# Batch 0 of an FFT filter ahead of an MLP: i moved into a second inverse table, angles by an integer shift, filters in three parts, another order

## The chip, the core and the metric

The kernel runs on one core of a Trainium2 chip. The metric is the device time of one execution in microseconds (us). The profile shows five engines: TensorE (PE in the profile, with its weight loads PEld), VectorE (DVE), ScalarE (ACT), GpSimd (POOL) and SyncE (SP). A program on one core has no second core to compare with, so each execution is judged by its time and by its mean granted TensorE clock, where 1.000 is full speed.

## The reference, cut to what matters

```python
x = randn(8, 3008, 256) * 0.1                     # batch, sequence, channels
F = filt_r + 1j * filt_i                          # (1505, 256)
y = irfft(rfft(x, axis=1) * F, n=3008, axis=1)    # a global filter along the sequence
h = y.reshape(24064, 256) @ w_in                  # 256 -> 2048
g = 0.5 * h * (1 + erf(h / sqrt(2)))
out = g @ w_out                                   # 2048 -> 256, fp32
```

## The kernel before

The Fourier transform of 3008 points is done by tables: 3008 = 47 x 64, so a first transform over 47 (table T1), a second over 64 with the twiddles in its table (T2), the product with the filter, and the way back (T3, T4). The tables are computed on the chip as sines. Batch 0 is transformed entirely in SBUF before the MLP can start (c1, c1t, c2, product, c3, c3t, c4); batches 1 to 7 are transformed in between the matmuls of the MLP (s1, r1, s2, s3, r2, s4, with a trip through DRAM). Here each engine works through its own instructions in the order in which the program lists them. Of the tiles named below, at is what c1 leaves, b its transposes (c1t), which c2 reads, p the filtered products, vt what c3 leaves, d its transposes (c3t), which c4 reads, and y the result; for batches 1 to 7, d is loaded back from DRAM (R).

The angles of T2 are kept in turns. The program brings them between -0.5 and 0.5 before the sine: they are rounded by adding and subtracting a large number, and the rounded part is subtracted:

```python
def table_2_angle(self, h):
    v, k = self.nc.vector, K1 // 2
    w, r = self.gen[:, h], self.gen[:, 2]
    if h == 0:
        v.scalar_tensor_tensor(out=w, in0=kk..., scalar=self.n2, in1=jn..., op0=ALU.mult, op1=ALU.add)
    else:
        v.tensor_scalar(out=w, in0=self.gen[:, 0], scalar1=self.n12, scalar2=None, op0=ALU.add)
    v.tensor_scalar(out=r, in0=w, scalar1=RND, scalar2=-RND, op0=ALU.add, op1=ALU.add)
    v.tensor_tensor(out=w, in0=w, in1=r, op=ALU.subtract)

def table_2_sin(self, h):
    self.nc.scalar.activation(out=self.T2[:, 12 * h:12 * h + 12, 1, :], in_=self.gen[:, h], func=AF.Sin, scale=2.0 * PI)
```

The second transform yields z, and the filter needs z*fr + (i z)*fi. T2 holds three blocks a row, so that c2 computes z and i z by two sets of matmuls in two PSUM banks; one VectorE instruction multiplies both by the two parts of the filter, and c3 adds the two halves by accumulating two matmuls with the same weights T3:

```python
def c2(self, p):
    ...
    for t, o in ((0, 1), (1, 0)):                  # z, then i z
        for i in range(2):
            k = 2 * p + i
            nc.tensor.matmul(ps[:, t, 256 * i:256 * i + 256], lhsT=self.T2[:, k, o:o + 2]...,
                             rhs=self.st[0, "b", k // 4][:, k % 4, :], start=True, stop=True)
    f = self.F[:, :, 2 * p:2 * p + 2, :]
    if p < 11:
        nc.vector.tensor_tensor(out=w, in0=ps, in1=f.rearrange("p t a b -> p t (a b)"), op=ALU.mult)
        return
    ...                                            # the last product in two halves

def c3(self, p, np=2):
    ...                                            # for t in (0, 1):
    self.nc.tensor.matmul(ps[half][:, c:c + 128], lhsT=w[:, t, o:o + 128],
                          rhs=self.T3[:, 2 * (p + i) + k]..., start=t == 0, stop=t == 1)
```

The filters come by DMA into the lower 64 partitions in parts of rows, and GpSimd (for the first rows VectorE) copies them to the upper 64. The order of the start-up, with cuts:

```python
m.load_x(0, 0, 1, (0,)); ...; m.load_x(0, 1, 4)    # x of batch 0
m.table_2(g); m.table_2_angle(0); m.unit_matrices(g, cols); m.table_2_angle(1)
for k, n in ((0, 4), (4, 4), (8, 8), (16, 8)):
    m.load_filters(k, n)
m.dup_filters(nc.gpsimd, 4, 4)
m.load_w_in()                                      # two large DMA issues between the copies
m.dup_filters(nc.gpsimd, 8, 8)
for u in range(16):
    m.c1(u // 2, u % 2, act if u < 4 or u % 2 else False)
    if u == 3:
        m.warm_up(3); m.table_2_sin(0)
    ...
nc.scalar.activation(out=warm, in_=m.p, func=AF.Gelu)   # brings the Gelu table
m.c1t(0, False); m.c1t(1, act)
...
m.c2(0); m.c2(1); m.table_3(0, act); m.table_2_swap(1); m.c1t(2, act)
for q in range(1, 7):
    ...                                            # c2, c1t, c2, tables, c3
m.psum(wide, v=(5, 1), t=(3, 1))                   # PSUM banks of c4 and c3t
for u in range(10):
    ...                                            # c3t(u), c4(u - 2)
...
# batches 2 to 7, in slots of the MLP counted back from the batch's first slot hi:
s1, n1, r1, s2, n2, r2, s4, n4 = hi - 94, 3.5, hi - 80, hi - 69, 3.5, hi - 24, hi - 17, 1
```

`warm_up(n)` is n matmuls on a tile of ones whose result nobody reads; they only keep TensorE busy.

## Time and profile before

| | before |
|---|---|
| time, median of 3 runs | 774.69 us (774.12 to 776.34) |
| span of the profiled execution | 772.2 us |
| first sine of T2 | 8.38 us |
| first filter product | 16.72 us |
| last product ends | 32.02 us |
| first matmul of the MLP | 40.55 us |

The page, the busy time by stretch and the main links of the start-up are in the prediction below. Here are four more lines of the timeline of the kernel before (columns: start us, length us, engine, line, operation, output<-input, shapes, count, and in brackets the idle time just before with what ended it):

```profile
5.75 1.01 DVE L179 SCALAR_TENSOR_TENSOR gen<-kk,n,jn 128x768 f32<-128x768 f32 x1
6.79 0.56 DVE L183 TENSOR_SCALAR gen<-gen 128x768 f32<-128x768 f32 x1
...
8.38 0.84 ACT L187 ACTIVATE T<-gen 128x768 bf16<-128x768 f32 x1 [0.18 <-DVE gen L184]
...
40.55 0.59 PE L461 MATMUL ps_h<-y_sb,w_in_sb 128*128 128x512 bf16 x2 [0.73 <-DMA x_sb<-in_x_dram]
```

The sine at 8.38 waits for the subtraction (L184). The MLP starts at 40.55; its wait is put down to a load of x, but the last eviction of y ends within the same 0.73 us.

### The profile page before, as it was taken

What the parts mean: (1) busy time and instruction counts of PE and PEld (TensorE: products, weight loads), DVE (VectorE), ACT (ScalarE), POOL (GpSimd) and SP (SyncE); (2) the same over time, 40 slices, a digit from 0 to 9 for tenths busy, and PEclk for the clock granted to TensorE, in tenths of its full rate; (3) what the DMA queues carried; (4) which work ended last, traced back from release to release, by engine and by line L of the source; (5) the groups of instructions that cost most, each with busy time, mean ns of one, the idle gap of its engine ahead of it and who ended that gap; (6) DMA issues with size and microseconds to landing.
All of it is one profiled execution on the core that took longest, in us unless ns stands there. A gap on an engine that the chain in (4) does not pass through costs nothing.

```text
span 772.2 us, 15059 instructions
## 1 busy us (share of the span) xinstructions
PE 763.2 (99%) x6066; PEld 528.7 (68%) x6066; DVE 397.3 (51%) x722; ACT 567.4 (73%) x981; POOL 64.9 (8%) x160
## 2 busy tenths in 40 slices
PE   8999999999999999999999999999999999999998
PEld 4847675676776766677777776666776776766666
DVE  7866755464555645457463664637646366411011
ACT  6879955897568975699656996579865798666663
POOL 7801100020000200011000110001100000000000
PEclk9999999999999999999999999999999999999999
DMA  8894745466253661636516464255553422410111
GB/s 138 145 180 124 150 123 129 128 124 151 57 139 107 138 159 41 192 78 122 143 53 181 85 133 123 79 154 95 124 137 81 139 83 69 123 42 28 42 42 55
DMA packets 87398, 85.66 MB, mean 111 GB/s; under 512 B 6752, under 2 KB 77536, under 8 KB 87328
## 3 DMA queue, kind: packets, MB, share of 16 engines
q1 hardware_dynamic: 78816, 68.70, 31.0%
q0 software_dynamic: 8512, 16.00, 14.9%
q8 instruction: 47, 0.77, 0.4%
q14 instruction: 23, 0.19, 0.1%
HBM read 54.00 MB, written 46.66 MB: 130 GB/s over the span
## 4 chain that ended last, share of the span: by engine, by line
PE 94%; DMA 3%; POOL 2%; issue 0%; DVE 0%; POOLq 0%
PE ps_o L488 43%; PE ps_h L461 42%; PE ps_s L345 2%; PE ps_s L320 2%; PE ps_s L295 2%; PE ps_s L272 2%; DMA x_sb<-in_x_dram 2%; POOL F L96 1%; POOL x_sb L82 1%; DMA F<-in_filt_i_dram 1%; POOL F L91 0%; PE ps_e L478 0%; POOL T1s L258 0%; DVE ost L501 0%; POOL T1p L580 0%
## 5 line engine op out<-in xcount | busy, mean ns | idle before, releaser
L464 ACT ACTIVATE g_sb<-ps_h 128x512 bf16<-128x512 f32 x752 | 438.0, 597 | 182.8 <-PE ps_h L461 172.1
L488 PE MATMUL ps_o<-w_out_sb,g_sb 128*128 128x256 bf16 x2992 | 447.5, 273 | 0.0
L461 PE MATMUL ps_h<-y_sb,w_in_sb 128*128 128x512 bf16 (+3 forms) x1600 | 445.8, 366 | 0.7 <-DMA x_sb<-in_x_dram 0.7
L488 PEld LDWEIGHTS <-g_sb 128*128 128x128 bf16 x2992 | 283.9, 98 | 134.3 <-issue 9.9
L461 PEld LDWEIGHTS <-w_in_sb 128*128 128x128 bf16 x1600 | 154.7, 98 | 23.7 <-issue 1.1
L494 DVE COPY ost<-ps_o 128x512 f32<-128x512 f32 x93 | 63.8, 686 | 143.5 <-PE ps_o L488 143.4
L303 DVE TENSOR_TENSOR p<-ps_s,F 128x512 bf16<-128x512 f32 x84 | 58.1, 691 | 105.9 <-ACT p L302 89.5
L249 DVE TENSOR_SCALAR y_sb<-ps_s 128x376 bf16<-128x376 f32 x112 | 60.9, 548 | 80.5 <-PE ps_s L345 80.5
L247 DVE CAST a_sb<-ps_s 128x512 bf16<-128x512 f32 x112 | 69.3, 682 | 27.7 <-PE ps_s L272 27.7
L247 DVE CAST v_sb<-ps_s 128x512 bf16<-128x512 f32 x84 | 57.4, 684 | 2.9 <-PE ps_s L320 2.6
L301 ACT ACTIVATE p<-ps_s 64x512 bf16<-64x512 f32 x84 | 49.9, 594 | 2.1
L302 ACT CAST p<-ps_s 64x512 bf16<-64x512 f32 x84 | 48.5, 577 | 1.0
L345 PEld LDWEIGHTS <-d_sb 96*128 96x128 bf16 x448 | 30.8, 97 | 25.3 <-DMA d_sb<-R 0.2
L101 POOL COPY gate<-p 1x1 bf16<-1x1 bf16 x48 | 8.5, 178 | 470.3 <-DVE p L305 470.3
L305 DVE TENSOR_TENSOR p<-p 128x512 bf16<-128x512 bf16 x84 | 35.7, 425 | 2.9
L345 PE MATMUL ps_s<-T,d_sb 96*128 96x94 bf16 x448 | 36.3, 204 | 0.0
L304 DVE TENSOR_TENSOR p<-p,F 128x512 bf16<-128x512 bf16 x84 | 34.8, 415 | 0.0
L82 POOL DMA_DIRECT2D x_sb<-in_x_dram x64 | 32.7, 512 | 13.0 <-issue 12.5
L320 PE MATMUL ps_s<-p,T 128*128 128x256 bf16 x168 | 32.1, 273 | 0.0
L295 PE MATMUL ps_s<-b_sb,T 128*128 128x256 bf16 x168 | 32.1, 273 | 0.0
L320 PEld LDWEIGHTS <-T 128*128 128x128 bf16 x168 | 16.4, 98 | 20.1 <-DVE p L305 0.5
L295 PEld LDWEIGHTS <-T 128*128 128x128 bf16 x168 | 16.4, 98 | 13.4
(103 smaller groups left out, 189.1 us busy)
## 6 DMA issues: line engine op xcount, KB each, us to landing
out_dram<-ost SPq DMA_DIRECT2D x93, 256.0 KB, 2.3
x_sb<-in_x_dram POOLq DMA_DIRECT2D x64, 188.0 KB, 3.8
R<-a_sb SPq DMA_DIRECT2D x112, 96.0 KB, 2.1
b_sb<-R SPq DMA_DIRECT2D x28, 384.0 KB, 4.3
R<-v_sb SPq DMA_DIRECT2D x42, 256.0 KB, 3.5
d_sb<-R SPq DMA_DIRECT2D x56, 192.0 KB, 4.7
w_in_sb<-in_moe_w_in_dram POOLq DMA_DIRECT2D x2, 512.0 KB, 7.8
w_out_sb<-in_moe_w_out_dram POOLq DMA_DIRECT2D x2, 512.0 KB, 11.3
```

The costliest lines, as they stand in the source:

```text
L247: self.nc.vector.tensor_copy(out=out, in_=in_)
L249: self.nc.vector.tensor_scalar(out=out, in0=in_, scalar1=scale, scalar2=None, op0=ALU.mult)
L295: nc.tensor.matmul(ps[:, 256 * i:256 * i + 256], lhsT=self.T2[:, k, 1:3].rearrange("p a b -> p (a b)"), rhs=self.st[b, "b", k // 6][:, k % ...
L301: nc.scalar.activation(out=p2[0:64], in_=ps[64:128], func=AF.Copy, scale=-1.0)
L302: nc.scalar.copy(out=p2[64:128], in_=ps[0:64])
L303: nc.vector.tensor_tensor(out=p1, in0=ps, in1=f(0), op=ALU.mult)
L320: nc.tensor.matmul(ps[:, 256 * i:256 * i + 256], lhsT=self.T3[:, k].rearrange("p a b -> p (a b)"), rhs=w[:, 256 * i:256 * i + 256], start= ...
L345: nc.tensor.matmul(ps[:, 94 * i:94 * i + 94], lhsT=d[:, (grp % 2) * 4 + i, 128 * half:128 * half + 128], rhs=t4, start=True, stop=True)
L461: nc.tensor.matmul(ps[:, o:o + n], lhsT=self.w_in_sb[:, dc, jc * 128:jc * 128 + 128], rhs=self.ring[:, dc, off:off + n], start=(dc == 0), ...
L464: nc.scalar.activation(out=self.st["g", t][:, jc, :], in_=ps, func=AF.Gelu)
L488: nc.tensor.matmul(ps[:, tile_i % 2, :], lhsT=g[:, jc, tile_i * 128:tile_i * 128 + 128], rhs=self.w_out_sb[:, jc, :], start=(jc == 0), sto ...
L494: nc.vector.tensor_copy(out=ost, in_=ps)
```

## The change

The intent is to shorten the start-up of 40.5 us. Five things change together.

1. Multiplying by i moves into a second inverse table T3i. Then c2 needs one set of matmuls, the product reads one PSUM bank twice, and c3 uses T3 for one half and T3i for the other.
2. Angles carry an extra 64 turns, which makes every value a float between 64 and 128. Shifting its bits left by 15 drops sign, exponent and the six bits of whole turns. What remains, read as a signed integer, is the fraction of a turn, and the sine takes it with the scale 2 pi / 2^32.
3. Filters come in parts of 4, 8 and 12 rows: 12 transfers instead of 16.
4. w_in is loaded ahead of all filter copies.
5. The order is another one, with more warm-up matmuls and the Gelu table brought later. The loads of x, too, stand elsewhere among GpSimd's instructions (not in the excerpt), but the last is issued at nearly the same time, 5.8 us against 5.9.

```diff
-        v.tensor_scalar(out=r, in0=w, scalar1=RND, scalar2=-RND, op0=ALU.add, op1=ALU.add)
-        v.tensor_tensor(out=w, in0=w, in1=r, op=ALU.subtract)
+        ts(out=self.gen[:, 1, k].bitcast(I32), in0=w[:, k].bitcast(I32), scalar1=15, scalar2=None,
+           op0=ALU.logical_shift_left)
 ...
-        self.nc.scalar.activation(out=self.T2[:, 12 * h:12 * h + 12, 1, :], in_=self.gen[:, h], func=AF.Sin,
-                                  scale=2.0 * PI)
+        self.nc.scalar.activation(out=self.T2[:, k, 0, :], in_=self.gen[:, 1, k].bitcast(I32), func=AF.Sin,
+                                  scale=2.0 * PI / 2.0 ** 32)
 ...
+    def table_3_copy(self, q, turn):
+        v = self.t3.rearrange("p (k n r) -> p k r n", k=8, r=2)
+        self._evac(self.T3[:, 8 * q:8 * q + 8], v, "act")
+        if turn:
+            for r in range(2):
+                self._evac(self.T3i[:, 8 * q:8 * q + 8, r, :], v[:, :, 1 - r, :], "act", self.turn[r])
 ...                                               # in c2
-        for t, o in ((0, 1), (1, 0)):
-            for i in range(2):
-                nc.tensor.matmul(ps[:, t, 256 * i:256 * i + 256], lhsT=self.T2[:, k, o:o + 2]..., ...)
+        for i in range(2):
+            nc.tensor.matmul(ps[:, 256 * i:256 * i + 256], lhsT=self.T2[:, k]..., ...)
-            nc.vector.tensor_tensor(out=w, in0=ps, in1=f..., op=ALU.mult)
+            nc.vector.tensor_tensor(out=w, in0=ps.unsqueeze(1).to_broadcast([128, 2, 512]), in1=f..., op=ALU.mult)
 ...                                               # in c3
+                        t3 = (self.T3i if t else self.T3)[:, 2 * (p + i) + k]
 ...                                               # in the order
-    for k, n in ((0, 4), (4, 4), (8, 8), (16, 8)):
+    for k, n in ((0, 4), (4, 8), (12, 12)):
         m.load_filters(k, n)
-    m.dup_filters(nc.gpsimd, 4, 4)
     m.load_w_in()
-    m.dup_filters(nc.gpsimd, 8, 8)
+    m.dup_filters(nc.gpsimd, 4, 20)
 ...
+    m.c1t(0, (act, False))
+    m.table_3_copy(1, True)
+    m.c1t(1, (act,))
+    m.c2(0)
+    m.warm_up(1)
+    m.c2(1)
+    m.c1t(2, (act,))
+    m.warm_up(2)
+    for q in range(1, 7):
+        ...                                        # c2, c1t, warm_up(2), c2, c3, warm_up(1)
 ...
-    m.psum(wide, v=(5, 1), t=(3, 1))
+    m.psum(wide, v=(4, 1), t=(4, 1))
```

## The prediction

> **What bounds the kernel now.** I read first the page (engine shares and the chain that ended last), then the busy time by stage, then the start-up by its timeline, its groups and its waits. The page:
>
> ```profile
> PE 763.2 (99%) x6066; PEld 528.7 (68%) x6066; DVE 397.3 (51%) x722; ACT 567.4 (73%) x981; POOL 64.9 (8%) x160
> ...
> PE 94%; DMA 3%; POOL 2%; issue 0%; DVE 0%; POOLq 0%
> ```
>
> TensorE is busy for 99% of the span and makes 94% of the chain. The table of stretches says where the rest lies (columns: stretch, its length, busy us of PE, PEld, DVE, ACT, POOL with instruction counts, TensorE clock, DMA share, GB/s):
>
> ```profile
> 0.00:10.00 10.00, 7.15 (x44) 3.46 (x45) 7.40 (x32) 4.41 (x9) 7.74 (x25) 1.00 0.75 128
> 10.00:20.00 10.00, 8.98 (x109) 6.52 (x106) 8.70 (x14) 9.22 (x19) 8.35 (x15) 1.00 1.02 149
> 20.00:30.00 10.00, 9.43 (x129) 8.61 (x129) 8.81 (x9) 9.36 (x16) 9.71 (x14) 1.00 0.82 143
> ...
> 100.00:300.00 200.00, 200.00 (x1600) 138.85 (x1598) 109.78 (x199) 146.56 (x252) 10.96 (x32) 1.00 0.50 120
> ```
>
> From 41 us on TensorE never stops (200.00 of 200). There the change touches nothing but the stride of a weight tile (T2 holds two blocks a row, not three). So 731.6 us of the 772.2 (first matmul of the MLP at 40.55 us to the end) stay as they are, and everything is decided in the first 40.5 us: building the tables and transforming batch 0. There no single engine is full; the timeline shows who holds whom:
>
> ```profile
> 14.53 0.89 PEld L371 LDWEIGHTS <-at_sb 128*128 128x128 bf16 x16 [0.66 <-DVE at_sb L247]
> ...
> 16.72 4.82 DVE L388 TENSOR_TENSOR p<-ps_c,F 128x1024 bf16<-128x1024 f32 x4
> ...
> 22.43 6.88 DVE L388 TENSOR_TENSOR p<-ps_c,F 128x1024 bf16<-128x1024 f32 x6 [0.88 <-POOL F L96]
> ...
> 29.61 1.23 DVE L388 TENSOR_TENSOR p<-ps_c,F 128x1024 bf16<-128x1024 f32 x1 [0.30 <-POOL F L96]
> ...
> 33.69 5.56 DVE L247 COPY d_sb<-ps_c3t 96x1024 bf16<-96x1024 bf16 x8 [0.75 <-PE ps_c3t L424]
> ```
>
> Three links. (a) To 14.5 us: the first transform (c1), paced by x arriving (its last part waits for DMA at 13.09). (b) 16.72 to 32.02: twelve filter products on VectorE, back to back but for 0.88 + 0.30 us in which they wait for GpSimd to copy the filters to the upper 64 partitions (L96, ten copies of 1.04 us). (c) 32.5 to 40.4: eight VectorE copies of 0.69 us, then two evictions, and the MLP starts.
>
> **What the Trainium skill says.** "VectorE: DVE Perf Modes", section "The perf-mode tier table": a two-tensor operation runs at one element a cycle with any PSUM operand; a one-source fp32 operation in SBUF reaches twice that. The trace agrees: the product of 1024 elements takes 1217 ns (1024 / 0.96 GHz = 1067, plus a fixed part), the two-source subtract of 768 fp32 959 ns, the one-source add 560. Hence reading one PSUM bank twice by a broadcast saves VectorE nothing. "ScalarE: Activation LUTs", section "What ACT_TABLE_LOAD costs": 1283 ns a load, and about 93 ns more for a per-partition scale. The load agrees (1283 ns at L571); for the second the trace has only a hint: the 94-column T4c eviction, with such a scale, takes 357 ns. "DMA: Bandwidth & Descriptors", section "Anatomy of one DMA": some 2 us fixed per transfer beside the bytes. Filter transfers of 64 KB here take 4.1 to 5.4 us from issue to landing, queueing included, so the trace is not against it.
>
> **The change part by part.**
> 1. *Products (c2).* The multiplication by i moves from the second table to the inverse one, so c2 needs 2 matmuls a pair of rows in place of 4: 24 fewer of 256 columns, some 0.3 us less per pair (four now take 0.60 us). About 20 extra warm-up matmuls are put between, at some 0.21 us each (three in 0.81-0.84 us at full clock, with latency). TensorE gains nothing net and isn't the bound here; VectorE's products are unchanged.
> 2. *Tables.* The two round-and-subtract pairs (0.56 + 0.96 us each) become one shift each; I take 0.56 us from the one-source row, so 1.9 us less VectorE before the sines. The first sine can start near 7.2 us, not 8.38. But x still lands near 13 us, so little comes out of it.
> 3. *ScalarE before the products.* Added ahead of 14.5 us: a table-3 copy (1.02) and two swaps (0.86); taken out: two evictions (0.9). It had 0.69 + 0.44 us of idle time after 9 us, so c1 ends at 14.5 to 15.2 instead of 14.5. The first c1t is split over two engines and only eight transposes stand before it, which gives back about 0.4. First product: 16.7 to 17.0 (now 16.72).
> 4. *Filters.* 12 transfers instead of 16 save 4 x 0.54 = 2.2 us of GpSimd issue, and no w_in issue stands between the copies. Rows 4 to 11 should be there by 17.5, the first copy done at 18.6, the tenth near 28 (now 29.3). At 1.04 us a copy against 1.15 a product (6.88/6) copies stay ahead: the waits of 0.88 + 0.30 go.
> 5. *ScalarE in the products.* Out: the table load and its dummy (1.48, to the idle 2.29 us before the c4 evictions), T1q 0.35, two minus copies and two swaps 1.63, T4c 0.36. In: four turned copies of 512 elements, 0.58 + 0.09, so about 2.6. The c1t for rows 4 to 7 now stands behind the second table-3 copy and two of them: 16.45 + 1.02 + 1.3 + 1.0 = 19.75, so the third product starts at about 20.2 where VectorE is free at 19.35. A new wait of about 0.85.
>
> Sum for the end of the products: 17.0 + 2.35 + 0.85 + nine at 1.15 + 1.2 = 31.75, against 32.02: -0.3. ScalarE's own sum (16.45 + 1.0 + 1.3 + three b 3.0 + vt 1.2 + b 1.0 + vt 1.2 + b 1.0 + table 3 2.3 + four vt 4.3) ends at 32.8 against 32.58 now, so it may hold the last vt: +0.1. Link (c) has the same VectorE work: 0. Net about -0.2 to -0.3, from 774.69 to 774.4.
>
> **The rivals.** *All waits of the products vanish* (c1 ends at 14.5, the c1t isn't late): VectorE is then the only bound, first product 16.3, end near 30.2, and 1.8 us are gained: 772.9. For it: VectorE loses 1.9 us before the sines. Against it: ScalarE is at 9.2 and 9.4 of 10 us already. *ScalarE becomes the bound*: the 2.6 us of turned copies aren't covered, c3 evictions come late and c3t starts 1 us later: 775.7. For it: the same two numbers; against it: as much was taken out. *The filters come late in coarse parts*: 12 rows must all land before the thirteenth is copied; if that is after 25 us the seventh product waits, up to +1 us. Against it: all filters were in by about 22 us even with 16 issues. *The long stage is disturbed*: no; weights, sizes, order and loads are the same there.
>
> **Range and chances.** 2% is 15.5 us, over a third of the whole start-up, and no rival moves over 2 us. The three runs of before spread over 2.2 us, so the range is the rivals' and about half a microsecond: 773.0 to 775.8.
>
> **What would show it.** Right: the MLP's first matmul at 40.0 to 40.9 us; no product waiting for GpSimd; product duration still 1.22 us; a wait of 0.5 to 1.2 us before the third product, released by TensorE after ScalarE's b; the shift at about 0.56 us; the second table load inside ScalarE's idle time; 731.6 us from first MLP matmul to the end. Wrong: a shift of 0.95 us, filters after 25 us, ScalarE's last vt after 33.3, or a long stage that differs by over 0.5 us, say from a single TensorE stop of its own.

## The result

Ratios here and below are the mean time of one kernel's fast runs over the mean of the other's of the same rounds, so they are not quite the ratio of the medians quoted. Before ran in 774.95 us (median of 4, 774.12 to 776.34), after in 773.71 (median of 4, 773.30 to 774.88). The ratio is 0.9985 with a 95% interval of 0.9966 to 1.0003: the same within 2%, and not told apart from no change at all.

The page of the kernel after:

```profile
span 771.8 us, 15050 instructions
PE 763.7 (99%) x6060; PEld 527.3 (68%) x6060; DVE 397.7 (52%) x734; ACT 568.3 (74%) x980; POOL 63.0 (8%) x154
```

The shares are those of before. The busy time by stretch of the kernel after (columns as in the prediction):

```profile
10.00:20.00 10.00, 8.11 (x99) 5.70 (x97) 8.28 (x16) 9.14 (x15) 7.97 (x14) 1.00 1.15 175
20.00:30.00 10.00, 9.91 (x129) 8.14 (x127) 9.34 (x10) 8.61 (x14) 9.77 (x15) 1.00 0.67 122
```

Between 20 and 30 us TensorE is now busy for 9.91 of 10, against 9.43 before: in the stage of the products it has next to no slack left. The timeline of the kernel after, by the same links as in the prediction:

```profile
6.07 0.61 DVE L182 TENSOR_SCALAR gen<-gen 128x768 int32<-128x768 int32 x1
6.71 0.84 ACT L208 ACTIVATE T<-gen 128x768 bf16<-128x768 int32 x1 [2.28 <-DVE gen L182]
...
14.10 0.90 PEld L395 LDWEIGHTS <-at_sb 128*128 128x128 bf16 x16 [0.42 <-DVE at_sb L271]
...
15.82 2.36 DVE L412 TENSOR_TENSOR p<-ps_c,F 128x1024 bf16<-128x1024 f32 x2
...
18.39 0.38 PE L408 MATMUL ps_c<-b_sb,T 128*128 128x256 bf16 x2 [1.27 <-ACT b_sb L269]
...
18.86 7.20 DVE L412 TENSOR_TENSOR p<-ps_c,F 128x1024 bf16<-128x1024 f32 x6 [0.68 <-PE ps_c L408]
...
26.58 3.49 DVE L412 TENSOR_TENSOR p<-ps_c,F 128x1024 bf16<-128x1024 f32 x3 [0.52 <-issue]
...
32.00 1.28 ACT L637 ACT_TABLE_LOAD   x1
...
32.92 5.56 DVE L271 COPY d_sb<-ps_c3t 96x1024 bf16<-96x1024 bf16 x8 [0.75 <-PE ps_c3t L445]
...
39.24 0.55 DVE L273 TENSOR_SCALAR y_sb<-ps_c 128x376 bf16<-128x376 f32 x1 [0.22 <-PE ps_c L459]
...
39.94 0.59 PE L482 MATMUL ps_h<-y_sb,w_in_sb 128*128 128x512 bf16 x2 [0.73 <-DVE y_sb L273]
```

The first product starts 0.9 us earlier than in the first trace of before (15.82 against 16.72). No product waits for GpSimd. Instead the third waits 0.68 us, because its matmuls wait for ScalarE's copy b, and the ninth 0.52 us. The six in between take 7.20 us, against 6.88 for six before. The chain of waits of the kernel after tells who sets that pace (columns: start us, length us, what):

```profile
20.75 0.22 PE ps_warm L263
...
21.64 0.43 PE ps_warm L263 x2
...
24.06 0.43 PE ps_warm L263 x2
```

From 19.2 to 31.7 us the chain is TensorE's nearly throughout, and ten entries of it, 3.03 us together, are warm-up matmuls.

### The profile page after: what moved, and what is told of

The parts are those of the page before. It is cut to its first block, busy times and chain, and to the rows that moved or that the text cites. A ratio compares the mean times of both kernels' runs of the same rounds, so it can differ in the third digit from the quotient of the medians.

```text
span 771.8 us, 15050 instructions
## 1 busy us (share of the span) xinstructions
PE 763.7 (99%) x6060; PEld 527.3 (68%) x6060; DVE 397.7 (52%) x734; ACT 568.3 (74%) x980; POOL 63.0 (8%) x154
## 4 chain that ended last, share of the span: by engine, by line
PE 97%; DMA 1%; DVE 1%; POOL 0%; ACT 0%; issue 0%; POOLq 0%; DVEq 0%; SPq 0%
PE ps_o L509 42%; PE ps_h L482 42%; PE ps_s L369 2%; PE ps_s L344 2%; PE ps_s L319 2%; PE ps_s L296 2%; DMA x_sb<-in_x_dram 1%; PE ps_c L430 1%; PE ps_c3t L445 0%; DMA d_sb<-R 0%; PE ps_warm L263 0%; POOL x_sb L83 0%; PE ps_c L408 0%; PE ps_c L459 0%; PE ps_c1t L395 0%; PE ps_e L499 0%
## 5 line engine op out<-in xcount | busy, mean ns | idle before, releaser
L482 PEld LDWEIGHTS <-w_in_sb 128*128 128x128 bf16 x1600 | 154.7, 98 | 23.7 <-issue 1.9
L83 POOL DMA_DIRECT2D x_sb<-in_x_dram x64 | 32.6, 511 | 13.3 <-issue 12.8
```

The costliest lines, as they stand in the source:

```text
L482: nc.tensor.matmul(ps[:, o:o + n], lhsT=self.w_in_sb[:, dc, jc * 128:jc * 128 + 128], rhs=self.ring[:, dc, off:off + n], start=(dc == 0), ...
```

## The experiments

Three calls of four kernels, each call on one chip, with the kernel before run in the same rounds. One profile of each gives the marks below. The first column is when the last of the eight loads of x for batch 0 landed, read from the landing records of the trace. The last column runs from the first matmul of the MLP to the start of the last group of matmuls in TensorE's timeline, so it is the long stage.

| kernel | last x lands | first product | MLP starts | in between | long stage |
|---|---|---|---|---|---|
| before | 12.95 | 16.72 | 40.55 | 23.83 | 726.74 |
| before again (b0_before) | 12.43 | 16.22 | 39.94 | 23.72 | 726.75 |
| after | 12.30 | 15.82 | 39.94 | 24.12 | 727.02 |
| after again (a0_again) | 12.77 | 16.27 | 40.39 | 24.12 | 726.89 |
| a1_nowarm | 12.74 | 16.20 | 39.39 | 23.19 | 727.88 |
| a2_late | 12.69 | 16.08 | 39.72 | 23.64 | 726.73 |
| a3_both | 12.77 | 16.26 | 39.43 | 23.17 | 728.61 |
| a5_parts | 12.02 | 15.73 | 40.04 | 24.31 | 727.06 |
| a6_float | 12.41 | 18.58 | 42.66 | 24.08 | 726.80 |
| s3_both_shift | 12.07 | 15.73 | 38.53 | 22.80 | 726.76 |
| a9_c1warm | 12.61 | 16.10 | 40.22 | 24.12 | 727.10 |
| b3_shift | 12.82 | 17.86 | 41.36 | 23.50 | 726.84 |
| s0_shift | 12.32 | 15.83 | 39.95 | 24.12 | 726.92 |
| s5_banks | 12.36 | 15.86 | 38.42 | 22.56 | 726.79 |

Two things stand out. The first product moves from 15.73 to 16.27 between kernels whose code up to there is the same or nearly so, so a difference under half a microsecond there need not be one of the code. The first column shows where it comes from: at full clock the first product starts 3.77 and 3.79 us after the last x in the two traces of before, and 3.39 to 3.71 us after it in those of the changed start-up. The time from issue to landing of these loads (the longest is the last number), as the view of x's tile gives it, in after and in a0_again, the same kernel:

```profile
DMA to landing us min/median/max: 3.7/5.1/6.5
```

```profile
DMA to landing us min/median/max: 3.6/5.6/7.0
```

The second is half a microsecond longer, and its first product comes 0.45 us later. The time in between repeats to 0.1 us (24.12 four times, twice with the very same kernel), so it tells kernels apart well.

My theory after the result was that the earlier start (from the shorter angle work and the filter parts) is real, and that the products then lose it to TensorE's warm-ups and to ScalarE's turned copies ahead of the third product. The rival was that nothing had been gained at the start, and that x's landing sets the first product in any case.

### a0_again: the changed kernel against itself on another chip, 5 rounds

No edit.

> The changed kernel itself, for a tighter ratio and a second trace. In the first traces the MLP's first matmul starts at 39.94 us against 40.55 before (0.61 us), the last TensorE matmul 0.33 us earlier. If the start-up is the whole of it, the ratio is 0.999 to 0.9995 and the start of the MLP is again 39.9 +- 0.1. If the 1.2 us between the medians is real and comes from the long stage too, the ratio is 0.9985 again and the length from first MLP matmul to the last matmul is shorter than before's 726.7 us.

Measured: 773.74 us (773.63 to 773.94, 5 runs) against 773.68 of before (773.46 to 774.48, 9 runs), ratio 0.9999 (0.9986 to 1.0011). All 14 executions had the clock 1.000. The timeline of this run:

```profile
16.27 2.36 DVE L412 TENSOR_TENSOR p<-ps_c,F 128x1024 bf16<-128x1024 f32 x2
```

The first product is now at 16.27, not 15.82, with x landed at 12.77 instead of 12.30. With undisturbed clocks there is no measurable gain.

### a1_nowarm: no warm-ups after the first transform

```diff
     m.table_3(1)
     m.dup_filters(nc.vector, 0, 4)
-    m.warm_up(1)
     m.c1t(0, (act, False))
...
-    m.warm_up(1)       # and the (2) or (1) after each c1t, c2 and c3 behind it
```

> All warm-up matmuls after the first transform taken out. Theory 1 (TensorE, filled with 3.0 us of warm-ups on its chain, has become the bound of the products after the third one): the 0.52 us wait before the ninth product goes, and the MLP starts 0.4 to 0.6 us earlier, at 39.4 to 39.5. Theory 2 (warm-ups lie in slack): within 0.1 us of 39.94. Theory 3 (the warm-ups keep the clock gate open): eight transposes take over 0.8 us instead of 0.61 somewhere, and the MLP starts over 0.5 us later.

Measured: 774.49 us (773.52 to 774.82), ratio 1.0006 (0.9993 to 1.0018); three of the five executions had clocks of 0.998 to 0.999. The timeline of the products, then TensorE's waits in the long stage (us in total, times, longest):

```profile
19.24 10.27 DVE L412 TENSOR_TENSOR p<-ps_c,F 128x1024 bf16<-128x1024 f32 x9 [0.68 <-PE ps_c L408]
```

```profile
PE ps_s L369 <- DMA d_sb<-R: 0.8, 2, 0.5
```

Nine products now run without a break at 10.27 / 9 = 1.14 us each: the wait of 0.52 and the slower six are gone, so both came from the warm-ups. First product to MLP falls from 24.12 to 23.19 us. But the time does not fall: the long stage is 1.0 us longer, of which 0.8 are two waits for loads of d: 0.5 near 285 us (the r2 step of batch 2) and 0.3 near 661 us.

### a2_late: ScalarE's turned copies behind the second set of b copies

```diff
     m.c1t(0, (act, False))
-    m.table_3_copy(1, True)
     m.c1t(1, (act,))
     m.c2(0)
     m.warm_up(1)
     m.c2(1)
     m.c1t(2, (act,))
+    m.table_3_copy(1, True)
```

> The second table-3 copy with its two turned copies moved behind the b evictions of rows 4 to 11 on ScalarE. Theory 1 (ScalarE's order alone makes the 0.68 us wait before the third product, as predicted): the wait goes to under 0.1 us, the MLP starts up to 0.6 us earlier unless TensorE's warm-ups hold it. Theory 2 (GpSimd's copy of rows 4 and 5, done at about 18.7 us because those filters land at 17.6, is right behind): the wait stays at 0.5 to 0.6 us, now released by GpSimd, and the MLP starts within 0.15 us of 39.94.

Measured: 772.93 us (772.64 to 773.22), ratio 0.9988 (0.9976 to 1.0001) to before. Against a0_again on the same chip, all five runs are below all five: 772.95 against 773.75 in the mean. The timeline:

```profile
18.63 4.61 DVE L412 TENSOR_TENSOR p<-ps_c,F 128x1024 bf16<-128x1024 f32 x4 [0.19 <-PE ps_warm L263]
24.10 5.75 DVE L412 TENSOR_TENSOR p<-ps_c,F 128x1024 bf16<-128x1024 f32 x5 [0.86 <-POOL F L97]
```

The wait before the third product falls from 0.68 to 0.19 us, so ScalarE's order had caused most of it. What is left ends with GpSimd's first filter copy, at 18.59 us, although the label names a warm-up; in after that copy ended at 18.70, 0.16 before the third product. So GpSimd stood right behind ScalarE, as the second theory had it. A part is given back: the products catch up with GpSimd and wait 0.86 us for a filter copy, which itself waited for filters that landed at 22.9 us.

### a3_both: both edits together

```diff
     m.c1t(0, (act, False))
-    m.table_3_copy(1, True)
     m.c1t(1, (act,))
     m.c2(0)
-    m.warm_up(1)
     m.c2(1)
     m.c1t(2, (act,))
-    m.warm_up(2)
+    m.table_3_copy(1, True)
...                                # and the other warm-ups of a1_nowarm
```

> Both: no warm-ups after the first transform and the turned copies late. If GpSimd's copy holds the third product, this equals the kernel without warm-ups within 0.15 us; if ScalarE alone does, the MLP starts at 38.8 to 39.0, about 1 us before the changed kernel.

Measured: 774.10 us (773.61 to 774.68), ratio 1.0002 (0.9988 to 1.0016), all clocks 1.000. The first six products run without a listed wait, and the MLP starts at 39.43. TensorE's waits in the long stage, and the loads of d near 283 us (columns: transfer, queue, kind, count, size, median us from issue to landing):

```profile
PE ps_s L369 <- DMA d_sb<-R: 1.2, 2, 1.0
```

```profile
d_sb<-R SPq DMA_DIRECT2D x8, 192.0 KB, 5.9
```

In a0_again the same loads took:

```profile
d_sb<-R SPq DMA_DIRECT2D x8, 192.0 KB, 4.7
```

The long stage is 1.7 us longer than in a0_again and 1.87 longer than in before. The view lists 1.2 us of it as waits for loads of d. The rest shows when the matmuls of the MLP are matched one by one with those of before: TensorE falls back by 0.30 us near 103 us, by 1.12 near 285 and by 0.41 near 662, each time at matmuls that read a loaded d. So in a1 and a3 the gain of the start-up was taken back at loads of d, most of it 240 us later. The totals did not fall as the start-ups did.

### b0_before: the kernel before once more

No edit; one look.

> The kernel before itself, for a second trace. Five traces of the changed code up to the first product had it start at 15.82 to 16.27 us, as x landed earlier or later. If before's start-up spreads as much, its first product starts at 16.5 to 17.0 and its MLP at 40.3 to 40.9; if its first trace (16.72, 40.55) was at one end, the start-up gain of the change is 0 or 1 us and not 0.2 to 0.6.

Measured: 773.33 us. The timeline:

```profile
16.22 4.84 DVE L388 TENSOR_TENSOR p<-ps_c,F 128x1024 bf16<-128x1024 f32 x4
21.81 6.88 DVE L388 TENSOR_TENSOR p<-ps_c,F 128x1024 bf16<-128x1024 f32 x6 [0.74 <-POOL F L96]
```

The first product of before, too, varies by half a microsecond from run to run (16.72 and 16.22). So the 0.9 us by which the two official traces differ is in part chance. The two traces of before average 16.47 and the nine profiles with the changed start-up (after, a0, a1, a2, a3, a5, s0, s3, s5) 15.98, half a microsecond earlier. But x had also landed 0.24 us earlier in the nine (12.45 against 12.69 in the mean), at times that overlap, and no run shows that the change did that. Counted from x's landing the changed code gains 0.25 us (3.53 against 3.78).

### a6_float: the changed kernel with the old rounding

```diff
-        ts(out=self.gen[:, 1, k].bitcast(I32), in0=w[:, k].bitcast(I32), scalar1=15, scalar2=None,
-           op0=ALU.logical_shift_left)
+        ts(out=self.gen[:, 1, k], in0=w[:, k], scalar1=RND, scalar2=-RND, op0=ALU.add, op1=ALU.add)
+        v.tensor_tensor(out=self.gen[:, 1, k], in0=w[:, k], in1=self.gen[:, 1, k], op=ALU.subtract)
...
-        self.nc.scalar.activation(..., in_=self.gen[:, 1, k].bitcast(I32), func=AF.Sin, scale=2.0 * PI / 2.0 ** 32)
+        self.nc.scalar.activation(..., in_=self.gen[:, 1, k], func=AF.Sin, scale=2.0 * PI)
```

> The changed kernel with round-and-subtract (two more VectorE instructions, about 0.56 and 0.96 us in place of one of 0.56) instead of the shift. Theory 1 (the shift is what lets the first transform's later parts run as x lands): the first sine starts 0.9 to 1.0 us later, near 7.7, and the first product 0.3 to 0.6 us later, near 16.6 to 16.8. Theory 2 (as predicted, x holds that stretch anyway): the first product at 16.1 to 16.4, MLP within 0.2 us.

Measured: 775.42 us (775.35 to 776.15), ratio 1.0017 (1.0003 to 1.0031). Three of four executions had the clock 1.000 and took 775.35 to 775.48, against 773.88 in the mean of five such executions of before in this call: 1.5 us more. The profiled execution was the fourth (clock 0.998). Its timeline and its busy time by stretch:

```profile
7.74 0.84 ACT L208 ACTIVATE T<-gen 128x768 bf16<-128x768 f32 x1 [3.28 <-DVE gen L183]
...
18.58 2.35 DVE L412 TENSOR_TENSOR p<-ps_c,F 128x1024 bf16<-128x1024 f32 x2
```

```profile
14.00:16.00 2.00, 2.00 (x27) 1.91 (x26) 1.85 (x6) 1.82 (x5) 2.00 (x4) 0.63 1.37 201
16.00:18.00 2.00, 2.00 (x19) 1.73 (x17) 0.82 (x2) 0.53 (x2) 1.94 (x5) 0.52 0.94 141
```

The first sine comes 1.0 us later than in the changed kernel, and the first product much later; in this execution TensorE also ran at about half clock within these 4 us (0.63, 0.52). Before the clock fell, the first transform had already stopped for VectorE, which was busy with the second half of the angles:

```profile
12.32 0.79 PE L385 MATMUL ps_c<-T1c,x_sb 94*128 94x96 bf16 x8 [0.77 <-DVE at_sb L271]
```

The three full-clock executions are 1.5 us slower than before, and 1.0 slower than a5_parts on the same chip, the nearest to the changed kernel there; none of them has a trace. In the kernel before the same two roundings, with the first sine at 8.38, still led to a first product at 16.2 to 16.7. So in the new order the old angles would stand on the path to the products, and the shift is what makes that order possible. That is not the same as a gain over before: there the first product follows x's landing, as I had predicted.

### a5_parts: filters in parts of 4, 4, 8 and 8 rows again

```diff
-    for k, n in ((0, 4), (4, 8), (12, 12)):
+    for k, n in ((0, 4), (4, 4), (8, 8), (16, 8)):
```

> The changed kernel with filters in parts of 4, 4, 8 and 8 rows as before, all else as changed. Theory 1 (coarse parts save 2.2 us of issue and make the copies earlier): the tenth GpSimd copy ends later than the 27.6 to 29.0 of the changed traces by 0.5 us or more, and products wait for GpSimd as before (0.9 to 1.2 us), MLP 0.5 us later. Theory 2 (the transfers' bytes set the landing, the parts don't matter): copies within 0.5 us, no product waits on GpSimd, MLP within 0.2 us.

Measured: 774.58 us (773.75 to 774.80), ratio 1.0002 (0.9988 to 1.0016); all clocks 1.000, where before's five such executions average 773.88 and these four 774.43. The timeline:

```profile
19.60 6.88 DVE L412 TENSOR_TENSOR p<-ps_c,F 128x1024 bf16<-128x1024 f32 x6 [1.51 <-POOL F L97]
```

GpSimd's first copy is finished later (19.57 us against 18.70), because it issues four more transfers first, and the third product waits 1.51 us for it. In the changed kernel that copy was in time. But the wait stands in the place of the 0.68 for ScalarE and of a part of the wait for TensorE, so from the first product to the MLP only 0.19 us are lost (24.31 against 24.12).

### s3_both_shift: a3 with most of the transform steps of batches 2 to 7 two slots earlier

```diff
-            s1, n1, r1, s2, n2, r2, s4, n4 = hi - 94, 3.5, hi - 80, hi - 69, 3.5, hi - 24, hi - 17, 1
+            s1, n1, r1, s2, n2, r2, s4, n4 = hi - 96, 3.5, hi - 82, hi - 71, 3.5, hi - 26, hi - 17, 1
```

> No warm-ups after the first transform, turned copies late, and in the long stage everything of batches 2 to 7 but the last transform two slots (1.7 us) earlier. The same without the shift started the MLP at 39.43 but took 774.1 us. Theory 1 (the gain of the start-up is given back where the loads of d of batch 2 land too late, 0.8 to 1.2 us of TensorE's waits near 285 us): these waits go, from first MLP matmul to the last matmul 726.6 to 726.9 us, time 772.6 to 773.0. Theory 2 (it is given back elsewhere, or in a varying way): 773.6 or more, with the length still over 727.5.

Measured: **772.32 us** (771.93 to 772.42), ratio 0.9974 (0.9960 to 0.9987), all clocks 1.000. The timeline:

```profile
15.73 6.89 DVE L412 TENSOR_TENSOR p<-ps_c,F 128x1024 bf16<-128x1024 f32 x6
22.90 5.75 DVE L412 TENSOR_TENSOR p<-ps_c,F 128x1024 bf16<-128x1024 f32 x5 [0.28 <-POOL F L97]
```

No wait for the loads of d is left, and the long stage is 726.76 us, that of before. So the missing gain of a3 lay in those loads, which now have two slots more before s4 reads them. This version is faster than before by an interval clear of one, though by a quarter of a per cent, and it stays so against before's five executions at full clock in this call (773.88 in the mean, against 772.19). From the first product to the MLP it takes 22.80 us, against 23.7 to 23.8 in before. The MLP starts at 38.53 instead of 39.94 to 40.55, but a part of that is x, which landed early here (12.07).

### a9_c1warm: no warm-ups within the first transform

```diff
         if u == 3:
-            m.warm_up(3)
...                     # u == 7: warm_up(2), u == 11: warm_up(1)
```

> The changed kernel without the three, two and one warm-up matmuls inside the first transform. With the rounding in place of the shift TensorE's granted clock fell to 0.63 and 0.52 between 14 and 18 us and the first product came at 18.58. Theory 1 (TensorE idling in the first transform lets its clock drop, and that is most of those 2.3 us): with these warm-ups gone the clock falls below 0.8 somewhere before 20 us, the first product starts at 17.0 or later. Theory 2 (the extra VectorE work itself is the cause): the clock stays 1.00 and the first product starts at 15.7 to 16.3.

Measured: 773.88 us (773.51 to 773.98), ratio 0.9997 (0.9985 to 1.0010). The profiled execution kept the clock 1.0 and had its first product at 16.10, like the changed kernel; two of the four executions had 0.998, at 773.51 and 773.96. So these warm-ups are worth nothing that this run can show; whether they keep the clock up in some executions is taken up below.

### b3_shift: the kernel before with the two slots alone

```diff
-            s1, n1, r1, s2, n2, r2, s4, n4 = hi - 94, 3.5, hi - 80, hi - 69, 3.5, hi - 24, hi - 17, 1
+            s1, n1, r1, s2, n2, r2, s4, n4 = hi - 96, 3.5, hi - 82, hi - 71, 3.5, hi - 26, hi - 17, 1
```

> The kernel before with batches 2 to 7 two slots earlier, alone. Theory 1 (the loads of d are only late where the start-up has been moved): the long stage stays at 726.6 to 726.9 us, and the time within 0.3 us of before. Theory 2 (the shift itself is a gain for any start-up): over 0.8 us faster.

Measured: 775.74 us (773.90 to 776.90, 6 runs), ratio 1.0021 (1.0007 to 1.0035). The two executions at the clock 1.000 took 773.90 and 774.20; the other four, at 0.995 to 0.997, took 774.84 to 776.90. The busy time by stretch of the profiled one (0.997):

```profile
5.00:10.00 5.00, 2.38 (x36) 1.67 (x36) 4.72 (x14) 2.73 (x6) 3.62 (x7) 1.00 0.99 172
10.00:12.00 2.00, 1.48 (x7) 0.61 (x6) 2.00 (x4) 1.97 (x5) 1.09 (x3) 0.74 1.02 194
12.00:14.00 2.00, 2.00 (x18) 1.54 (x18) 1.23 (x3) 1.25 (x3) 1.40 (x3) 0.50 1.21 180
14.00:16.00 2.00, 1.83 (x25) 1.23 (x24) 1.02 (x2) 1.20 (x3) 2.00 (x5) 0.90 0.85 106
```

The clock fell to half from about 11 to 14 us, in a start-up whose code is the same as before's, and the first product slipped to 17.86. Of before's own executions in this call 4 of 11 also had a clock below 1.000, without a trace. The long stage is 726.84, so the shift of slots alone gives nothing here. The longer total goes with the clock, not with the shift: its two executions at full clock are close to before's seven of this call (773.58 to 774.07).

### s0_shift: the changed kernel with the two slots alone

The same two lines of edit, on the changed kernel.

> The changed kernel with the two slots' shift alone. Its second trace had one TensorE wait of 0.2 us for a load of d. Theory 1: faster than the changed kernel by 0.1 to 0.4 us only, 773.3 to 773.7 us where before is at 773.7 to 774.2; the long stage 726.6 to 726.8. Theory 2 (the shift is most of the 1.9 us that the combined kernel gained): 772.7 or less.

Measured: 773.52 us (773.33 to 774.18), ratio 0.9995 (0.9983 to 1.0007). In between 24.12, long stage 726.92, as in the changed kernel. The shift gains only where the start-up was made faster (a3 to s3).

### s5_banks: s3 with the PSUM banks of the last stage as before

```diff
-    m.psum(wide, v=(4, 1), t=(4, 1))
+    m.psum(wide, v=(5, 1), t=(3, 1))
```

> The combined kernel (no warm-ups after the first transform, turned copies late, shift) with the PSUM banks of the last batch-0 stage as before, five and three in place of four and four. In the changed kernels the last y eviction waits 0.22 us for TensorE and the stretch from the last product's end to the MLP is 8.68 us, against 8.53 before. Theory 1 (the fifth bank): the wait goes, the stretch is 8.5 to 8.55 and the MLP starts 22.65 us after the first product, not 22.80. Theory 2 (something else): 8.68 again.

Measured: 772.51 us (771.89 to 772.89), ratio 0.9980 (0.9968 to 0.9992). The timeline:

```profile
37.11 1.17 DVE L273 TENSOR_SCALAR y_sb<-ps_c 128x376 bf16<-128x376 f32 x2
38.42 0.38 PE L482 MATMUL ps_h<-y_sb,w_in_sb 128*128 128x512 bf16 x1 [0.73 <-DVE y_sb L273]
```

From the last product to the MLP it takes 8.52 us, as in before (8.53 and 8.52), against 8.68 in after and a0_again. The last two evictions of y again run back to back (1.17 us), where after had a gap of 0.22 between them: with four banks instead of five the last matmuls of c4 came 0.22 us late. In the total so little cannot be told from the spread: 772.51 here, 772.32 in s3, on different chips.

### What the clock does

On one chip all 9 executions of before were at 1.000. On the two others 8 of 20 were below, at 774.71 us in the mean, against 773.83 for the 21 at full clock on all three; the longest was 776.36 at 0.995. Of the changed kernel's 9 executions (4 official, 5 of a0_again) none was below; they took 773.82 us in the mean. **At full clock, then, no difference between the two kernels shows in the mean**, with single runs spread over 1.6 us and the chips mixed; on the one chip that ran both (a0_again) it is 0.08 us. The median gain of 1.24 us in the official rounds is not a gain of the undisturbed kernel; the clocks of those executions of before are not on record, apart from the profiled one (773.98 at 1.000).

The low clock falls in the start-up in both traces that caught it (a6_float and b3_shift). The clock by single microseconds is 0.99, 0.50, 0.50, 0.50 and 0.81 from 10 to 15 us in b3_shift, and 0.76, 0.50, 0.50 and 0.53 from 14 to 18 us in a6_float. Taking it as either 0.50 or 1.00 at any moment, I estimate that it is low from 10.98 to 14.38 us and from 14.52 to 17.94, for 3.4 us each time. In both, TensorE was busy less than usual ahead of it: in b3_shift 2.38 of the 5 us up to 10 us (it waited 1.69 us for x), where the traces of before have 3.61 and 3.15 and the changed kernel has 4.30 and 4.17; in a6_float 1.34 of the 2 us up to 14 us, where before has 1.84 and 1.92 and the changed kernel 2.00 and 1.89. The Trainium skill, "TensorE: Matmul & The Clock Gate", section "What's actually happening", states that the clock is half by default and is released by activity in a window of about 3.4 us that runs freely, so that it differs from run to run. The two drops agree with that in depth (0.50) and in length. So does the start: in every trace the first warm-up matmuls begin 0.43 us apart and later ones 0.21 to 0.22, although the clock column says 1.00 there. By these distances the step comes near 4.2 us in b3_shift and near 4.3 in a6_float (an estimate), and the falls follow 6.8 and 10.2 us later, twice and three times 3.4. Two traces are few to build on. That more warm-ups keep the changed kernel from it is possible but not shown: of the kernels with all of the first transform's warm-ups and the shift, 38 executions had no drop, but a1_nowarm, which has them too, had three in five; a9_c1warm without them had two in four, a6_float one in four. The chips differ as well.

## Why the prediction was right or wrong, point by point

The total (774.4, between 773.0 and 775.8, the same within 2%) holds: 773.71. That is partly luck, because terms were wrong in opposite directions.

**The start, right in kind, its sum wrong.** "x still lands near 13 us so little comes out of it" holds: x landed at 12.0 to 12.8, and the first product follows its landing. Counted from there, c1 ends (the transposes c1t begin) 1.81 us after x in the mean of the changed traces, against 1.58 and 1.61 in before: 0.2 later, within the predicted 0 to 0.7. From c1t to the first product it takes 1.72 us in every changed trace at full clock, against 2.19 and 2.18: 0.46 is given back where the split c1t stands, predicted about 0.4. What failed is the addition. c1's end at 14.5 to 15.2, before's 2.19 and the 0.4 given back make 16.3 to 17.0; I wrote 16.7 to 17.0, as if c1 had to come at least 0.4 late. With x at 12.95, as in the trace that I reckoned from, the measured mean of 3.53 us after x gives an estimate of 16.48. The 15.73 to 16.27 measured are lower still only because x landed earlier in those executions. The shift's part in this is that the new order loses nothing (a6_float). No run takes back the split of c1t, the second table or the place of w_in alone, so their parts rest on these marks.

**The products, wrong.** The step that failed was "TensorE gains nothing net and isn't the bound here". From the third product on I had reckoned nine at 1.15 us and 1.2, which is 11.55; the trace has 12.40 from 18.86 to 31.26. The mis-sized term is the warm-ups' place: by duration they replace the matmuls saved, but they stand in TensorE's order right ahead of what VectorE waits for, and TensorE rose to 9.91 of 10. Without them (a1_nowarm) first product to MLP takes 0.93 us less.

**The wait before the third product, right in kind, a little large.** Predicted 0.85, released by TensorE after ScalarE's b; measured 0.68, and it goes when the turned copies move (a2_late).

**GpSimd's waits, right.** The 0.88 and 0.30 of before are gone. The first copy ended at 18.70 us, predicted 18.6, and the tenth at 27.65, predicted near 28; but the first was only 0.16 ahead of its product. a5_parts shows the coarser parts are what pays for it: with four parts the third product waits 1.51 for GpSimd.

**The shift, right.** 0.61 and 0.56 us, predicted 0.56. **The table load, right:** 1.28 us at 32.00; with the dummy behind it ScalarE is free at 33.50, and the first matmuls of c4 start only at 33.73. **The product's duration, right:** 1.22 us. **The turned copies, right:** the prediction cites the Trainium skill, "ScalarE: Activation LUTs", "What ACT_TABLE_LOAD costs", for about 93 ns more with a per-partition scale, for which the trace of before had only a hint. In after such copies of 512 elements took 686 and 694 ns in the mean, and one with an immediate scale 597: 89 to 97 ns more.

**The last link, slightly wrong.** I put it at zero. It is 0.15 us longer by the fourth bank that c4 gave to c3t, which s5_banks gives back.

**The long stage, right for the change,** 727.0 against 726.7. But I had called its disturbance impossible ("no; weights, sizes, order and loads are the same there"). a1_nowarm and a3_both, which change nothing but the start-up, lengthen it by 1.0 and 1.7 us, at matmuls that read a loaded d; the 0.28 of after is lost at such a one, too, near 101 us. Why the loads of d are late there stays open; s3_both_shift shows only that two slots of slack cure it.

In sum, by the table's marks: 0.5 us earlier at the first product, half of that by x, 0.3 to 0.4 later from there to the MLP (24.12 against 23.83 and 23.72), and 0.15 to 0.3 later in the long stage. In between, the two new waits (0.68 and 0.52) take the place of GpSimd's two (0.88 and 0.30; 0.74 and 0.30); the slower pace behind the warm-ups and the last link (0.15) make the rest. That leaves nothing, and the full-clock means show nothing.

## What to carry to other kernels

When a start-up is a chain over several engines, taking one wait away can hand the path to the next engine in line, as it did here: count for each engine of the stage how near it already is to full, filler work included, and look where the filler stands in the engine's order. A gain at the start must be followed to the end of the kernel, as a later stage that was just in time can take it back. With differences of a tenth of a per cent, compare executions by their granted clock before comparing kernels, and count the marks of a start-up from the landing of its input, which moved by 0.9 us here between executions.

## What the Trainium skill lacked or had wrong

- "TensorE: Matmul & The Clock Gate", "What's actually happening", lets the half clock come back after at least one idle window of about 3.4 us. If idle means without work, b3_shift differs: from 5 to 11 us TensorE was busy for 2.38 of the first five us and 0.70 of the last, so all its gaps there add up to 2.92, and the clock fell at 11.0.
- The same section puts the ramp's penalty under 1% of a typical kernel and advises not to fit a count. The size agrees (up to 2.5 us of 774 in before and 2.9 in b3_shift, 0.4%), but at this level it is larger than the whole change.
- "VectorE: DVE Perf Modes", "The perf-mode tier table", has times for bf16 and fp32 and none for int32. A logical shift of 768 int32 elements with an immediate took 0.56 and 0.61 us, the time of a one-source fp32 operation of that size (0.56).
